# Loading the first key tiles through transposing DMAs instead of transposing them on the matrix engine

## The chip, the cores and the metric

The kernel runs on one core of one Trainium2 chip. The metric is the device time of one execution in microseconds (us); a time below is the median of several executions. The time contains about 1.8 us outside the profiled span (before: 179.15 us for a span of 177.4 us in the profiled run).

Engine names: PE is the matrix engine (PEld is its weight load, which overlaps PE), DVE the vector engine, ACT the scalar engine, POOL the general one, SP the engine that issues most DMAs. A q behind a name (SPq) means its sequencer.

## The reference, cut to what matters

The input x has 2048 tokens of 512 features. A linear-attention block and a gated feed-forward block run on the same x and are mixed by a gate:

```python
qkv = x @ wqkv                              # 32 heads of 16
pq, pk = phi(q), phi(k)                     # phi(t) = where(t > 0, t + 1, exp(t)) + 1e-6
kv  = einsum("bhsd,bhse->bhde", pk, v)      # a sum over all 2048 tokens
z   = pk summed over the tokens
a   = (pq @ kv) / (pq . z + 1e-6) @ wo
b   = (silu(x @ w1) * (x @ w3)) @ w2
out = g * a + (1 - g) * b                   # g = sigmoid(x . gate_w)
```

The kernel does not compute v for every token. It sums XP = x^T phi(k) over the tokens and multiplies by wv afterwards. So x is needed in two layouts: feature-major (`xT`), as the weights side of the key, query and feed-forward matmuls, and token-major (`x_sb`), as the weights side of the XP matmuls. Nothing of the query or feed-forward part can be finished before the keys of all 16 tiles of 128 tokens are through, so the kernel starts with the keys.

## The kernel before: the parts that matter

The start works like this. Token-major x of tiles 0-1 comes first, as a copy. PE transposes these two tiles itself (eight matmuls against an identity), DVE and ACT copy the result to `xT`. All other tiles get `xT` by a transposing DMA. The first half of wk is issued on ACT's queue, so that it is under way at the same moment as x.

```python
    TF = 2
    x_first = x2d[0 : TF * P, :].rearrange("(p j) d -> p j d", j=TF)
    dq.dma_start(out=x_sb[:, 0:TF, :], in_=x_first)
    nc.scalar.dma_start(out=wk_sb[:, 0:2, :], in_=wqkv_r[:, 0:2, D : 2 * D])
    dq.dma_start(out=wk_sb[:, 2:4, :], in_=wqkv_r[:, 2:4, D : 2 * D])
    dq.dma_start(out=xT[:, :, TF * P : TB], in_=x2d[TF * P : TB, :], transpose=True)
    for tb in range(1, NTB):
        dq.dma_start(out=xT[...tiles of tb...], in_=x2d[...], transpose=True)
        dq.dma_start(out=x_sb[...], in_=x_r[...])
    # ... (wq, wr, wv, w1, w3, wo, w2 in this order on the same queue)

    emit_warm(TB, TB, TB, TB, TB, TB, P, P, P)      # matmuls on constants while the loads run
    # ...
    emit_xT(0); emit_xT(1)                           # PE transposes
    for kc, t in ((0, 0), (1, 0), (0, 1), (1, 1), (2, 0), (3, 0)):
        emit_k_mm(k0[t], t, kc)                      # first wk half for tiles 0 and 1 first
    # ... (rest of key tiles 0-3)
    for t in range(TPB, NT):                         # key tile t behind XP of tile t-4
        for u in range(n_xp, n_xp + (2 if t == NT - 4 else 1)):
            emit_xp(u, XP_ps)
            n_xp = u + 1
        emit_k(t)
```

A key tile is four matmuls of 128x512 into one PSUM tile, then phi: exp on ACT, two instructions on DVE. XP of a tile is four matmuls.

## Time and profile before

| | before |
|---|---|
| median of six executions | 179.93 us (179.27 to 180.15) |
| span of the profiled run | 177.4 us |
| PE busy | 172.9 us, 97% |
| first key matmul / first XP matmul | 4.56 us / 8.03 us |

The page's first part (busy us, share of the span, instructions) and the first line of its fourth part (the chain of waits that ended last) say that PE is the limit from one end to the other:

```profile
PE 172.9 (97%) x868; PEld 83.7 (47%) x884; DVE 117.7 (66%) x203; ACT 65.9 (37%) x124; POOL 63.2 (36%) x71
...
PE 97%; issue 1%; DVE 0%; DVEq 0%
```

So only two things can move the time: PE's work itself, and the moments at which PE cannot go on. The timeline of PE's first 9 us (start, duration, engine, line, what it writes and reads, how often; in brackets the idle time before it and what ended it):

```profile
0.84 3.04 PE L163 MATMUL warm<-const-bfloat16-1.0 128*128 128x512 bf16 x9 [0.84 <-PEq L473]
3.89 0.62 PE L176 MATMUL xTp<-ident,x_sb 128*128 128x128 bf16 x8
4.56 3.63 PE L186 MATMUL k<-wk_sb,xT 128*128 128x512 bf16 x16
8.03 1.03 PE L206 MATMUL XP<-pk_sb,x_sb 128*128 128x512 bf16 x4
```

The 16 key matmuls of tiles 0-3 start at 4.56 and XP follows at 8.03: 3.47 us, or 0.217 us from one matmul to the next. There is no hole. (The duration that the line shows for the group, 3.63 us, is 0.16 us longer than this: it runs to the end of the last matmul.)

The waits of PE's weight loads:

```profile
PEld L176 <- DMA x_sb<-in_A_x_dram: 0.3, 1, 0.3
PEld L186 <- DMA xT<-in_A_x_dram: 0.2, 1, 0.2
PEld L186 <- DVE xT L181: 0.2, 1, 0.2
PEld L206 <- DMA x_sb<-in_A_x_dram: 0.2, 1, 0.2
```

SP's issues in the first 7 us, then the time from issue to landing of four of the loads (the DMA view, each taken for the stretch in which the load was issued; the columns are what, queue, kind, how many, size, us to landing):

```profile
0.81 0.40 SPq L84 DMA_DIRECT2D x_sb<-in_A_x_dram  x1
1.27 0.41 SPq L86 DMA_DIRECT2D wk_sb<-in_A_wqkv_dram  x1
1.73 1.32 SPq L89 DMA_TRANSPOSE xT<-in_A_x_dram  x1
3.10 2.77 SPq L93 DMA_TRANSPOSE xT<-in_A_x_dram  x1
```

```profile
wk_sb<-in_A_wqkv_dram ACTq DMA_DIRECT2D x1, 256.0 KB, 3.6
x_sb<-in_A_x_dram SPq DMA_DIRECT2D x1, 256.0 KB, 3.0
wk_sb<-in_A_wqkv_dram SPq DMA_DIRECT2D x1, 256.0 KB, 4.0
xT<-in_A_x_dram SPq DMA_TRANSPOSE x1, 4.4
```

Here a copy of 256 KB holds SP for 0.40 to 0.41 us and lands 3.0 to 4.0 us after its issue began. A transposing DMA of two tiles holds SP for 1.32 us.

The trace has records of the clock that PE was granted. In this run the first record says full clock from 3.76 us on. Until then the matmuls of 512 columns start 0.43 us apart, afterwards 0.216 us: PE begins at half clock.

### The profile page before, as it was taken

The page shows a single profiled execution, that of the slowest core. Times are in us where ns is not written, and L with a number is a line of the kernel's source. Part 1 is how long each engine was busy: PE and PEld are TensorE (multiplying, and loading weights), DVE is VectorE, ACT ScalarE, POOL GpSimd, SP SyncE. Part 2 cuts the span into 40 slices and gives each one's busy share as a digit, 9 for nine tenths or more (in the row PEclk, how much of TensorE's full clock was granted, in tenths as well). Part 3 has the DMA queues.
Part 4 walks back from the last instruction along what each step waited for, and adds up shares of the span by engine and source line. Part 5 has one row for each costly group of instructions (what it writes and reads, how often), then busy time and mean ns, then how long its engine had stood idle before and what let it go on. Part 6 is the DMA issues. An engine that isn't in the chain of part 4 may idle for free.

```text
span 177.4 us, 2453 instructions
## 1 busy us (share of the span) xinstructions
PE 172.9 (97%) x868; PEld 83.7 (47%) x884; DVE 117.7 (66%) x203; ACT 65.9 (37%) x124; POOL 63.2 (36%) x71
## 2 busy tenths in 40 slices
PE   8999999999999999999999999999999999999993
PEld 3444444474445454444454544444545444444463
DVE  0596858898998637597876466978754668776000
ACT  3624324466433333333244333243434323341222
POOL 5197655958262323262003232710032328000000
PEclk9999999999999999999999999999999999999999
DMA  5999889951014011124000111230002022200011
GB/s 172 237 265 238 253 273 348 358 171 28 9 30 91 7 41 37 37 59 89 0 4 7 41 33 38 70 79 6 0 7 67 7 70 59 59 0 0 30 36 56
DMA packets 30252, 15.14 MB, mean 85 GB/s; under 512 B 20672, under 2 KB 30112, under 8 KB 30240
## 3 DMA queue, kind: packets, MB, share of 16 engines
q1 hardware_dynamic: 29968, 14.72, 30.8%
q10 hardware_dynamic: 272, 0.26, 0.4%
q8 instruction: 7, 0.11, 0.3%
q14 instruction: 5, 0.04, 0.1%
HBM read 8.42 MB, written 2.10 MB: 59 GB/s over the span
## 4 chain that ended last, share of the span: by engine, by line
PE 97%; issue 1%; DVE 0%; DVEq 0%
PE o_ps L357 19%; PE up_ps L320 19%; PE gate_ps L312 19%; PE o_ps L348 8%; PE XP L206 8%; PE q_ps L219 8%; PE k_ps L186 6%; PE r_ps L243 3%; PE k L186 2%; PE o_ps L352 2%; PE warm L163 2%; PE kvT_ps L418 1%; PE W_ps L440 0%; PE z_ps L431 0%; DVE xT L181 0%
## 5 line engine op out<-in xcount | busy, mean ns | idle before, releaser
L312 PE MATMUL gate_ps<-xT,w_sb 128*128 128x512 bf16 x157 | 40.7, 379 | 0.1
L320 PE MATMUL up_ps<-xT,w_sb 128*128 128x512 bf16 x157 | 40.6, 379 | 0.2
L227 POOL TENSOR_TENSOR qz<-pq,z_sb 128x512 f32<-128x512 bf16 x16 | 18.5, 1163 | 59.6 <-DVE pq L147 58.4
L325 ACT ACTIVATE th<-gate_ps 128x512 bf16<-128x512 f32 x40 | 23.9, 597 | 37.9 <-PE gate_ps L312 36.4
L357 PE MATMUL o_ps<-w_sb,hT 128*128 128x512 bf16 (+3 forms) x177 | 37.3, 355 | 0.2
L327 DVE SCALAR_TENSOR_TENSOR gs<-th,gate_ps 128x512 bf16<-128x512 bf16 x40 | 27.3, 683 | 5.6 <-ACT th L325 5.3
L330 DVE TENSOR_TENSOR hT<-up_ps,gs 128x512 bf16<-128x512 f32 x40 | 27.6, 691 | 3.7
L144 DVE TENSOR_SCALAR phi_m<-phi_e 128x512 bf16<-128x512 bf16 x32 | 14.1, 442 | 21.4 <-ACT phi_e L142 21.4
L357 PEld LDWEIGHTS <-hT 128*128 128x128 bf16 x180 | 16.8, 98 | 17.9
L320 PEld LDWEIGHTS <-w_sb 128*128 128x128 bf16 x160 | 15.6, 98 | 18.9
L312 PEld LDWEIGHTS <-w_sb 128*128 128x128 bf16 x160 | 15.6, 98 | 18.6
L362 ACT ACTIVATE o_out<-o_ps,omg 128x512 bf16<-128x512 f32 (+2 forms) x17 | 11.2, 659 | 30.8 <-PE o_ps L357 30.8
L292 POOL TENSOR_TENSOR pqn<-pq,rden 128x512 bf16<-128x512 bf16 x16 | 16.6, 1058 | 14.0 <-DVE rden L285 11.7
L196 POOL TENSOR_TENSOR pks<-pks,pk_sb 128x512 f32<-128x512 f32 x15 | 17.4, 1162 | 7.3 <-DVE pk_sb L147 6.7
L348 PE MATMUL o_ps<-W_sb,pqT 128*128 128x512 bf16 (+3 forms) x70 | 16.7, 354 | 0.1
L230 DVE TENSOR_REDUCE den<-qz 128x32 f32<-128x512 f32 x16 | 11.0, 685 | 8.6 <-POOL qz L227 8.5
L206 PE MATMUL XP<-pk_sb,x_sb 128*128 128x512 bf16 x62 | 16.2, 379 | 0.1
L219 PE MATMUL q_ps<-wq_sb,xT 128*128 128x512 bf16 x61 | 16.1, 379 | 0.1
L142 ACT ACTIVATE phi_e<-k_ps 128x512 bf16<-128x512 f32 x12 | 7.2, 597 | 14.4 <-PE k_ps L186 14.4
L142 ACT ACTIVATE phi_e<-q_ps 128x512 bf16<-128x512 f32 x16 | 9.6, 597 | 7.8 <-PE q_ps L219 6.7
L186 PE MATMUL k_ps<-wk_sb,xT 128*128 128x512 bf16 x48 | 12.3, 379 | 0.0
L147 DVE SCALAR_TENSOR_TENSOR pq<-q_ps,phi_m 128x512 bf16<-128x512 f32 x16 | 11.1, 691 | 0.5
(59 smaller groups left out, 116.7 us busy)
## 6 DMA issues: line engine op xcount, KB each, us to landing
w_sb<-in_B_w_dram SPq DMA_DIRECT2D x6, 640.0 KB, 8.8
out_dram<-o_out SPq DMA_DIRECT2D x15, 128.0 KB, 1.9
x_sb<-in_A_x_dram SPq DMA_DIRECT2D x2, 512.0 KB, 5.4
x_sb<-in_A_x_dram SPq DMA_DIRECT2D x1, 768.0 KB, 5.4
wq_sb<-in_A_wqkv_dram SPq DMA_DIRECT2D x1, 512.0 KB, 6.9
wv_sb<-in_A_wqkv_dram SPq DMA_DIRECT2D x1, 512.0 KB, 5.8
wo_sb<-in_A_wo_dram SPq DMA_DIRECT2D x1, 512.0 KB, 10.3
wk_sb<-in_A_wqkv_dram ACTq DMA_DIRECT2D x1, 256.0 KB, 3.6
```

Of the source, the lines that this page charges most:

```text
L186: nc.tensor.matmul(k_ps[:], lhsT=xT[:, kc, t * P : (t + 1) * P], rhs=wk_sb[:, kc, :], start=(kc == 0), stop=(kc == KC - 1),)
L196: nc.gpsimd.tensor_add(pks[:], pks[:], pk_sb[:, t, :])
L206: nc.tensor.matmul(XP_ps[dc][:], lhsT=x_sb[:, t, dc * P : (dc + 1) * P], rhs=pk_sb[:, t, :], start=(t == 0), stop=(t == NT - 1),)
L219: nc.tensor.matmul(q_ps[:], lhsT=xT[:, kc, ts_tok], rhs=wq_sb[:, kc, :], start=(kc == 0), stop=(kc == KC - 1),)
L227: nc.gpsimd.tensor_tensor(out=qz[:], in0=st[tb, "pq"][:, tt, :], in1=z_sb[:], op=ALU.mult)
L312: nc.tensor.matmul(gate_ps[:], lhsT=w1_sb[:, kc, fsl], rhs=xT[:, kc, tok_sl], start=(kc == 0), stop=(kc == KC - 1),)
L320: nc.tensor.matmul(up_ps[:], lhsT=w3_sb[:, kc, fsl], rhs=xT[:, kc, tok_sl], start=(kc == 0), stop=(kc == KC - 1),)
L325: nc.scalar.activation(out=th[:], in_=gate_ps[:], func=ACT.Tanh, scale=0.5)
L327: nc.vector.scalar_tensor_tensor(out=gs[:], in0=th[:], scalar=1.0, in1=gate_ps[:], op0=ALU.add, op1=ALU.mult)
L330: nc.vector.tensor_tensor(out=st[tb, "hT"][:, fc, :], in0=up_ps[:], in1=gs[:], op=ALU.mult)
L348: nc.tensor.matmul(o_ps[:], lhsT=st[tb, "pqT"][:, c, tsl], rhs=W_sb[:, c, a:b], start=(c == 0), stop=False,)
L357: nc.tensor.matmul(o_ps[:], lhsT=st[tb, "hT"][:, fc, tsl], rhs=w2_sb[:, fc, a:b], start=False, stop=(fc == FC - 1),)
```

## The change

The intent: no PE transposes, no identity, no copies out of PSUM for them. One queue (SP's) loads everything, in the order in which it is needed: tile 0 transposed, wk in two halves, tile 1 and tiles 2-3 transposed, then token-major x. Because token-major x now comes late, XP of tiles 0-3 is moved behind key tile 3, and key tiles 4, 5, 6 follow without XP between. Some later weight loads are merged.

```diff
-    dq.dma_start(out=x_sb[:, 0:TF, :], in_=x_first)
-    nc.scalar.dma_start(out=wk_sb[:, 0:2, :], in_=wqkv_r[:, 0:2, D : 2 * D])
-    dq.dma_start(out=wk_sb[:, 2:4, :], in_=wqkv_r[:, 2:4, D : 2 * D])
-    dq.dma_start(out=xT[:, :, TF * P : TB], in_=x2d[TF * P : TB, :], transpose=True)
-    for tb in range(1, NTB):
-        # ... xT of four tiles, then token-major x of four (the first time six) tiles
+    load_xT(0, 1)
+    for kcs in (slice(0, 2), slice(2, 4)):
+        dq.dma_start(out=wk_sb[:, kcs, :], in_=wqkv_r[:, kcs, D : 2 * D])
+    load_xT(1, 2)
+    load_xT(2, 4)
+    load_x(0, 2)
+    load_x(2, 4)
+    load_xT(4, 8)
+    load_x(4, 8)
+    load_xT(8, 12)
+    load_x(8, 16)
+    load_xT(12, 16)
     # ... (w3 and w2 in one DMA each instead of two)
-    emit_warm(TB, TB, TB, TB, TB, TB, P, P, P)
+    emit_warm(TB, TB, TB, TB, TB, TB, TB)
     # ... (emit_xT is gone)
-    # ... (key tiles 0 and 1 begun with the first wk half)
+    for t in range(TPB):
+        emit_k(t)
     XP_ps = [...]
-    n_xp = 0
+    for t in range(TPB):
+        emit_xp(t, XP_ps)
+    n_xp = TPB
     for t in range(TPB, NT):
-        for u in range(n_xp, n_xp + (2 if t == NT - 4 else 1)):
-            emit_xp(u, XP_ps)
-            n_xp = u + 1
+        if t >= TPB + 3:
+            emit_xp(n_xp, XP_ps)
+            n_xp += 1
         emit_k(t)
```

## The prediction

> **What bounds the kernel now.** The profile's engine table has the matrix engine (PE) busy 172.9 of 177.4 us (97%); DVE is next, 66%. The chain that ended last is PE for 97%. The waits view shows four waits of PE's weight loads on another engine or a DMA, 0.9 us together. So only PE's work, or when PE can start and go on, moves the time.

> **The start, by the timeline.** Nine warming matmuls 0.84 to 3.88; x of tiles 0-1 (issued 0.81) lands at 3.8; eight transposes from 3.89; first key matmul 4.56; key tiles 0-3 end at 8.19. The first wk half, on ACT's queue at 0.80, lands at 4.4, the second at 5.3.

> **Removed.** Eight PE transposes with the wait for their copies (3.89 to 4.56: 0.67 us), two DVE copies of 292 ns, two ACT copies of about 380 ns, the identity. The other matmuls keep their number. The warming now ends at about 3.85, as before.

> **Added and moved.** The wk halves now stand behind a transposing DMA on one queue. Issuing a transposing DMA of one 128x512 tile takes 1.22 us (pqT, SP's timeline), data moves after that for 0.8 us, and it lands 2.4 us after the issue began. A copy of 256 KB is issued in 0.41 us and lands 3.0 to 4.0 us after it, two others in flight. My estimate from these: issues at 0.81 (xT 0), 2.1 and 2.5 (wk), 3.0 (xT 1), 4.3 (xT 2-3), 5.6 and 6.2 (x), 6.8 (xT 4-7). Landings: xT 0 3.4; wk 4.7 and 5.3; xT 1 5.6; xT 2-3 7.1; x 0-1 8.4; xT 4-7 about 10.7. Key tiles 0-1 then end at about 6.6 (a hole of 0.8 us before the first, a small one between the halves), tiles 2-3 start at 7.1 and end at about 8.85: 0.65 us later than before. The saved transposes are inside that.

> XP of tiles 0-3 runs 8.85 to 12.3; xT 4-7 is there by then. Key tiles 4, 5, 6 follow without XP between, and XP of tile 4 comes two key tiles (1.73 us) after key tile 4; phi takes 0.60 (ACT) + 0.29 + 0.69 (DVE) and about 0.2 us between, sometimes over 2 us: a stall of 0.1 to 0.4 us. Later PE's order is the same.

> **Later loads.** The queue runs 1 to 2 us later. wq (landed 23.2, used 29.6), w1/w3 (used 37.9) and wo (used 41.6) have time to spare; merged w3 and w2 loads cost nothing.

> **Sum.** +0.65 + 0.25 - 0.2 (the x_sb wait before XP of tile 2 goes) = +0.7: **180.7 us, 8 in 10 between 179.9 and 182.2**. Faster by over 2%: 0.01; within 2%: 0.95; slower by over 2%: 0.04.

> **What would show it.** PE idle 3.85 to about 4.7, released by the wk DMA; a hole before key tile 2, released by xT; key tile 3 ending at 8.5 to 9.5; a short wait for pk before XP of tile 4; no DMA wait after 13 us; PE busy about 0.6 us less, span 0.7 more.

> **What would make it wrong.** The wk copies might start only when the transposing DMA has drained (between later xT and x loads the trace shows about 0.6 us of nearly idle DMA): +0.6. [...] here full clock begins at 3.76 us. [...] if they cool PE, early key tiles take twice as long: +1.5 us.

The sum, +0.65 + 0.25 - 0.2 = +0.7 us, stands as it was put on record; no term of it is cut. "They" are the holes that the changed start leaves in PE's work. The +1.5 us is the author's estimate. By the trace of before (0.43 us from one matmul to the next until 3.76 us, 0.216 us afterwards) it is what seven key matmuls at half clock would cost.

## More of the kernel before

The weight load of XP of tile 2 waits 0.20 us and starts at 11.35 us; XP of tile 2 starts at 11.48 us, which is 8.03 us plus exactly 16 matmuls of 0.216 us.

## The result and the profile after

| | before | after |
|---|---|---|
| median of six executions | 179.93 us (179.27 to 180.15) | 182.25 us (181.1 to 182.7) |
| ratio | | 1.0128 (95% interval 1.009 to 1.0166) |
| span of the profiled run | 177.4 us | 180.9 us |
| PE busy | 172.9 us | 174.4 us |
| first key matmul / first XP matmul | 4.56 / 8.03 us | 5.43 / 11.37 us |

A ratio here is the mean time of one kernel's runs over the mean of the other's runs of the same rounds, so it is not quite the ratio of the medians quoted beside it.

The change is slower, by 1.3%, and the measured 182.25 us lies just outside the predicted range of 179.9 to 182.2 us. PE is busy for longer than before although eight transposes are gone. The two lines of the page that answer to those above:

```profile
PE 174.4 (96%) x858; PEld 83.3 (46%) x874; DVE 116.7 (65%) x201; ACT 65.4 (36%) x122; POOL 63.2 (35%) x69
...
PE 94%; DMA 2%; SPq 1%; issue 1%; DVE 0%; DVEq 0%
```

A DMA and SP's sequencer are now on the chain that ended last. The timeline of PE shows where:

```profile
0.84 3.03 PE L164 MATMUL warm<-const-bfloat16-1.0 128*128 128x512 bf16 x7 [0.84 <-PEq L453]
5.43 0.59 PE L173 MATMUL k_ps<-wk_sb,xT 128*128 128x512 bf16 x2 [1.55 <-DMA wk_sb<-in_A_wqkv_dram]
6.33 0.59 PE L173 MATMUL k_ps<-wk_sb,xT 128*128 128x512 bf16 x2 [0.31 <-DMA wk_sb<-in_A_wqkv_dram]
7.15 4.38 PE L173 MATMUL k_ps<-wk_sb,xT 128*128 128x512 bf16 x12 [0.23 <-DMA xT<-in_A_x_dram]
11.37 3.62 PE L193 MATMUL XP<-pk_sb,x_sb 128*128 128x512 bf16 x16
```

There are three holes: one in front of the first key matmul, one between the wk halves, one in front of key tile 1. And there is something that is not a hole. The last twelve key matmuls take from 7.15 to 11.37 us, 4.22 us, where twelve of 0.216 us would be 2.59 us. Between 7.15 and 10.5 us they start 0.43 us apart: half clock again.

The loads: SP's issues, then from issue to landing for xT of tile 0, the wk halves, xT of tile 1, and xT of tiles 2-3.

```profile
0.81 1.29 SPq L82 DMA_TRANSPOSE xT<-in_A_x_dram  x1
2.15 1.08 SPq L91 DMA_DIRECT2D wk_sb<-in_A_wqkv_dram  x2
3.28 2.55 SPq L82 DMA_TRANSPOSE xT<-in_A_x_dram  x2
```

```profile
xT<-in_A_x_dram SPq DMA_TRANSPOSE x1, 2.7
...
wk_sb<-in_A_wqkv_dram SPq DMA_DIRECT2D x1, 256.0 KB, 3.2
...
wk_sb<-in_A_wqkv_dram SPq DMA_DIRECT2D x1, 256.0 KB, 3.5
...
xT<-in_A_x_dram SPq DMA_TRANSPOSE x1, 3.8
...
xT<-in_A_x_dram SPq DMA_TRANSPOSE x1, 3.6
```

So xT of tile 0 is there at 3.51 us, but the wk halves land at 5.39 and 6.29 us (4.42 and 5.25 before), xT of tile 1 at 7.10 and of tiles 2-3 at 8.08 us.

The granted clock, by windows chosen at the trace's clock records (full from 3.63, half from 7.05, full from 10.46 us; each stretch is 3.41 us long; the columns are length, then busy us and count of PE, PEld, DVE, ACT and POOL, then the clock, the DMA share and GB/s):

```profile
0.22:3.63 3.41, 2.79 (x7) 0.96 (x8) 0.17 (x1) 1.49 (x2) 1.97 (x9) 1.00 0.21 45
3.63:7.05 3.42, 1.43 (x5) 0.32 (x4) 0.00 (x0) 0.09 (x1) 0.00 (x0) 1.00 0.98 235
7.05:10.46 3.41, 3.31 (x8) 1.19 (x9) 1.71 (x4) 1.10 (x2) 0.61 (x1) 0.50 1.08 217
10.46:13.87 3.41, 3.41 (x17) 1.57 (x16) 2.70 (x5) 1.19 (x2) 1.97 (x2) 1.00 0.92 221
```

In the first window PE was busy for 82% and got the full clock for the next one. In the second it was busy for 42%, because of the holes, and got half clock for the third. The third was full of matmuls, and full clock came back. (The view prints 1.00 for the first window, which has no record yet; the spacing of 0.43 us shows that it was half.)

With this the two profiled spans can be compared piece by piece. Each piece is a difference of start times in the two timelines:

| piece | us |
|---|---|
| first key matmul later: 5.43 against 4.56 | 0.87 |
| hole between the wk halves: second matmul done at 5.86, third starts at 6.33 | 0.47 |
| hole before key tile 1: fourth done at 6.76, fifth starts at 7.15 | 0.39 |
| half clock: 4.22 us for twelve matmuls instead of 2.59 | 1.63 |
| first XP matmul to first query matmul: 21.75 us (11.37 to 33.12) against 21.58 (8.03 to 29.61); from there to the end both take 147.8 us | 0.17 |
| sum | 3.53 |
| difference of the spans, 180.9 - 177.4 | 3.5 |

The medians differ by 2.3 us only. This execution of the changed kernel was among its slowest (182.64 us), and this one of before among its fastest (179.15 us). How much of that spread is the clock, the experiments show in part.

### The profile page after: what moved, and what is told of

Same layout as the page of the kernel before. It is cut to its first block, busy times and chain, and to the rows that moved or that the text cites. A ratio compares the mean times of both kernels' runs of the same rounds, so it can differ in the third digit from the quotient of the medians.

```text
span 180.9 us, 2426 instructions
## 1 busy us (share of the span) xinstructions
PE 174.4 (96%) x858; PEld 83.3 (46%) x874; DVE 116.7 (65%) x201; ACT 65.4 (36%) x122; POOL 63.2 (35%) x69
## 4 chain that ended last, share of the span: by engine, by line
PE 94%; DMA 2%; SPq 1%; issue 1%; DVE 0%; DVEq 0%
PE up_ps L307 19%; PE o_ps L344 19%; PE gate_ps L299 19%; PE k_ps L173 8%; PE XP L193 8%; PE o_ps L335 8%; PE q_ps L206 8%; PE r_ps L230 3%; DMA xT<-in_A_x_dram 2%; PE o_ps L339 2%; SPq L82 1%; SPq L91 1%; PE kvT_ps L398 0%; PE W_ps L420 0%; DVE o_out L353 0%
## 5 line engine op out<-in xcount | busy, mean ns | idle before, releaser
L312 ACT ACTIVATE th<-gate_ps 128x512 bf16<-128x512 f32 x40 | 23.9, 597 | 37.9 <-PE gate_ps L299 36.4
L145 DVE TENSOR_SCALAR phi_m<-phi_e 128x512 bf16<-128x512 bf16 x32 | 13.6, 424 | 29.0 <-ACT phi_e L143 28.8
L173 PE MATMUL k_ps<-wk_sb,xT 128*128 128x512 bf16 x63 | 17.5, 410 | 2.1 <-DMA wk_sb<-in_A_wqkv_dram 1.9
L143 ACT ACTIVATE phi_e<-k_ps 128x512 bf16<-128x512 f32 x16 | 9.6, 597 | 22.1 <-PE k_ps L173 22.1
L173 PEld LDWEIGHTS <-xT 128*128 128x128 bf16 x64 | 6.6, 104 | 11.7 <-issue 4.3
```

The source lines that it names most:

```text
L143: e_ins = nc.scalar.activation(out=e[:], in_=ps, func=ACT.Exp)
L173: nc.tensor.matmul(k_ps[:], lhsT=xT[:, kc, t * P : (t + 1) * P], rhs=wk_sb[:, kc, :], start=(kc == 0), stop=(kc == KC - 1),)
L312: nc.scalar.activation(out=th[:], in_=gate_ps[:], func=ACT.Tanh, scale=0.5)
```

## The experiments

Theory: the change loses twice. Its loads arrive later (wk stands behind a transposing DMA, xT of tile 1 behind both), and the holes that this tears open keep PE at half clock or put it back there. Rivals: the loads alone; the new order of XP; the use of one queue, with or without transposing DMAs.

### The changed kernel again

No edit. Six executions.

> The changed kernel again, unedited, for its spread. Theory (loads late[...]): times fall in two groups, about 182.6 us where the profile shows a half-clock stretch of 3.4 us in the first 12 us, and about 181.1 to 181.9 us where it shows none; ratio to before 1.007 to 1.015. Rival (the whole loss is the late loads and the order of XP, the clock stretch is a by-product of the profiler): one group, no relation of the time to the granted clock.

Measured: 182.31 us (181.31 to 182.7), ratio 1.0138 (1.0109 to 1.0167). The twelve executions of the changed kernel are not in two groups; they fill the range from 181.1 to 182.7 us. The mean granted clock does not tell them apart either: it is 0.999 for one of 182.7 us. So both expectations failed in form. The trace of that execution says why. It has no clock record before 10.06 us, and its key matmuls start 0.43 us apart until then:

```profile
0.00:3.24 3.24, 2.40 (x6) 0.90 (x7) 0.17 (x1) 1.49 (x2) 1.98 (x9) 1.00 0.18 40
3.24:6.65 3.41, 1.86 (x5) 0.46 (x4) 0.00 (x0) 0.00 (x0) 0.00 (x0) 1.00 0.97 225
6.65:10.06 3.41, 3.41 (x9) 1.17 (x8) 1.21 (x3) 1.20 (x2) 0.61 (x1) 1.00 0.91 234
```

### More warming matmuls, no load moved

```diff
-    emit_warm(TB, TB, TB, TB, TB, TB, TB)
+    emit_warm(*[TB] * 14)
```

> The changed kernel with 14 warming matmuls instead of 7, so that PE is busy until about 5.35 us, when the first wk half lands; no load is moved. If the half-clock stretch comes from PE's hole of 1.55 us before the first key matmul, no execution shows it, key tile 3 ends at about 9.8 us, and the time is 181.0 to 181.5 us in every execution: 1.5 us under the changed kernel's slow group, the same as its fast group. Rival (loads alone): no change from the changed kernel.

Measured: 181.04 us, four executions within 180.98 to 181.07; ratio 1.0073 (1.0048 to 1.0099). The executions of the unedited changed kernel in the same job average 182.19 us, so filling the hole is worth 1.16 us on average, with every load as it was. The profile has no half-clock stretch after 5.16 us:

```profile
0.84 5.30 PE L164 MATMUL warm<-const-bfloat16-1.0 128*128 128x512 bf16 x14 [0.84 <-PEq L453]
5.99 3.86 PE L173 MATMUL k_ps<-wk_sb,xT 128*128 128x512 bf16 x16
9.68 2.54 PE L193 MATMUL XP<-pk_sb,x_sb 128*128 128x512 bf16 x11
```

The warming delays the first key matmul to 5.99 us, but that costs nothing: key tile 1 starts at 7.08 us, on the landing of its xT, as it did in the changed kernel (7.15). XP starts at 9.68 us. The first rival (loads alone) falls, and so does the rival that the profiler makes the half-clock stretch: the executions themselves became faster. The spread is gone as well.

### A hole in the kernel before, no load moved

```diff
-    emit_warm(TB, TB, TB, TB, TB, TB, P, P, P)
+    emit_warm(TB, TB, TB)
```

> The kernel before with three warming matmuls instead of nine: PE idles from about 2.1 to 3.9 us, no load and no other work is moved. If a hole before the first work costs clock time by itself, the full clock comes later (first key tiles with 0.43 us from one matmul to the next) and the time rises by 1 to 2.5 us over before, to 181 to 182.3 us, spread by execution. Rival (the hole costs nothing as long as the loads are the limit): 179.8 us as before.

Measured: 181.39 us (181.07 to 181.55) beside 179.25 us for before; ratio 1.0112 (1.0088 to 1.0136). This is the clock alone: the loads of the start land within 0.25 us of before's, the first key matmul is even at 4.53 us, and still XP starts 2.27 us later, at 10.30 instead of 8.03 us.

```profile
0.84 1.44 PE L163 MATMUL warm<-const-bfloat16-1.0 128*128 128x512 bf16 x3 [0.84 <-PEq L473]
3.70 1.03 PE L176 MATMUL xTp<-ident,x_sb 128*128 128x128 bf16 x8 [1.42 <-DMA x_sb<-in_A_x_dram]
4.53 5.93 PE L186 MATMUL k<-wk_sb,xT 128*128 128x512 bf16 x16
10.30 1.03 PE L206 MATMUL XP<-pk_sb,x_sb 128*128 128x512 bf16 x4
```

The hole of 1.4 us stands where nothing could have run. What it costs is paid later: the 16 key matmuls took 5.77 us instead of 3.47, with full clock only from 9.20 us on.

### The order of XP alone undone

```diff
-    for t in range(TPB):
-        emit_xp(t, XP_ps)
-    n_xp = TPB
+    n_xp = 0
     for t in range(TPB, NT):
-        if t >= TPB + 3:
-            emit_xp(n_xp, XP_ps)
-            n_xp += 1
+        for u in range(n_xp, n_xp + (2 if t == NT - 4 else 1)):
+            emit_xp(u, XP_ps)
+            n_xp = u + 1
         emit_k(t)
```

> The changed kernel with before's order of XP and key tiles (XP of tile t-4 in front of key tile t). The theory puts 0.25 us on the new order (the wait of XP of tile 4 for phi of key tile 4 at 17.2 us goes): time 0 to 0.3 us under the changed kernel, same two groups. Rival (the new order is the main loss): the time falls by 1 us or more. XP of tiles 0-1 may instead wait for token-major x, which lands at about 10 us: that would show before the first XP matmul.

Measured: 182.68 us (182.6 to 182.89), ratio 1.0164 (1.0134 to 1.0193): about 0.5 us slower than the unedited changed kernel, not faster. XP of tile 0 does not wait, but key tile 4 does, for 1.02 us:

```profile
10.43 1.03 PE L193 MATMUL XP<-pk_sb,x_sb 128*128 128x512 bf16 x4
12.48 1.04 PE L173 MATMUL k_ps<-wk_sb,xT 128*128 128x512 bf16 x4 [1.02 <-DMA xT<-in_A_x_dram]
```

In the new load order xT of tiles 4-7 lands late (12.76 us in the changed kernel's profile), and the 16 XP matmuls behind key tile 3 are what hides that. So the new order is not the loss; it is part of what keeps the loss small. It may also be why these four executions hardly differ: key tile 4 waits for that landing (12.43 us in this profile) whether the key tiles before it were fast or slow. My expectation of a small gain had looked only at the wait of XP of tile 4 that the order makes (0.25 us expected, 0.17 us measured).

### Both wk halves on ACT's queue

```diff
+    for kcs in (slice(0, 2), slice(2, 4)):
+        nc.scalar.dma_start(out=wk_sb[:, kcs, :], in_=wqkv_r[:, kcs, D : 2 * D])
     # ... (pre, load functions)
     load_xT(0, 1)
-    for kcs in (slice(0, 2), slice(2, 4)):
-        dq.dma_start(out=wk_sb[:, kcs, :], in_=wqkv_r[:, kcs, D : 2 * D])
```

> The changed kernel with both wk halves issued on ACT's queue at 0.8 us, as before did with the first half; xT stays alone on SP's. If the loss is wk standing behind a transposing DMA on one queue: first key matmul at about 4.5 us instead of 5.43, key tile 1 not waiting until 7.1, key tiles 0-3 ending at about 8 to 8.5 us (11.53 in the changed kernel's profile), no half-clock stretch, time 180.0 to 180.5 us. Rival (the loss is transposing x of tiles 0-3 by DMA at all, on whatever queue): xT still lands as late, key tile 3 still ends after 9.7 us, time over 181 us.

Measured: 181.36 us, with two executions at 180.44 and 180.54 and two at 182.17 and 182.66; ratio 1.0097 (1.0049 to 1.0145). The first wk half now lands at 3.60 us. But the first key matmul is no earlier: it starts at 5.62 us, for now xT of tile 0 is what comes late.

```profile
0.84 3.03 PE L164 MATMUL warm<-const-bfloat16-1.0 128*128 128x512 bf16 x7 [0.84 <-PEq L453]
5.62 3.63 PE L173 MATMUL k_ps<-wk_sb,xT 128*128 128x512 bf16 x16 [1.74 <-DMA xT<-in_A_x_dram]
9.08 1.24 PE L193 MATMUL XP<-pk_sb,x_sb 128*128 128x512 bf16 x5
```

After that there is no hole, so XP starts at 9.08 us instead of 9.68 (the filled kernel), and the two fast executions are 0.5 us under the filled kernel's 181.0. The hole in front has become longer, 1.74 us, and executions over 182 us are there again. In the profiled execution this hole lost no clock: all 16 key matmuls are 0.216 us apart. No execution over 182 us was profiled here, so their half clock is inferred, from the experiment that fills this hole too (below). The expectation was wrong about the first key matmul, and the reason was new: the packets of xT of tile 0 had moved by 3.67 us, but its completion came at 5.57 us. The second wk half ran beside it on the other queue and completed at 4.98 us. The next experiment tests whether that half held it up.

### Only the first wk half on ACT's queue

```diff
+    nc.scalar.dma_start(out=wk_sb[:, 0:2, :], in_=wqkv_r[:, 0:2, D : 2 * D])
     # ...
     load_xT(0, 1)
-    for kcs in (slice(0, 2), slice(2, 4)):
-        dq.dma_start(out=wk_sb[:, kcs, :], in_=wqkv_r[:, kcs, D : 2 * D])
+    dq.dma_start(out=wk_sb[:, 2:4, :], in_=wqkv_r[:, 2:4, D : 2 * D])
```

> The changed kernel with only the first wk half on ACT's queue at 0.8 us; the second stays on SP's behind xT of tile 0. In e1_wk_act the data of xT of tile 0 had moved by 3.67 us, but its completion came at 5.57, after that of the second wk half (4.98), which ran beside it on ACT's queue. If it is that copy which holds the completion up, xT of tile 0 now lands at 3.6 to 4.2 us, the first key matmul starts at 3.9 to 4.3 (5.62 in e1), with a hole of about 0.7 us before the second half (landing at 5.3 or so); key tile 3 still ends at 9 to 9.7 us, because xT of tile 1 (issued at 2.7) and tiles 2-3 come late. Time 180.5 to 181.5 us. Rival (any copy beside a transposing DMA delays it, whatever the order): xT of tile 0 lands after 5 us again.

Measured: 180.73 us (180.58 to 180.84), ratio 1.0059 (1.0032 to 1.0087). The DMA view of the stretch in which both were issued, first with both halves on ACT's queue, then with one:

```profile
xT<-in_A_x_dram SPq DMA_TRANSPOSE x1, 4.8
```

```profile
xT<-in_A_x_dram SPq DMA_TRANSPOSE x1, 3.3
```

The packets of tile 0 had moved at the same moment in both (3.65 and 3.67 us), yet it is complete at 4.13 us here and at 5.57 us there. In the trace 32 packets of 4 bytes follow the tile's data. Here they start at 3.13 to 3.65 us, there only at 4.18 to 4.36 us, while the copy's data ends at 4.35 us. From the last data packet to completion it takes 0.48 us with the copy issued later, 1.90 us with the copy running beside. So I take it that the second wk half on the other queue held the tile up, at least for a part; by what means, these two runs do not show. Nor do they show that it is all: there the copy itself was complete at 4.98 us, and the 0.59 us from then to 5.57 us stay open. The edit also moved xT of tile 1 away, which there is issued 1.33 us behind tile 0. Where it is issued as close behind without a copy on another queue ("wk in front of xT of tile 0", below), the time from last packet to completion is 0.76 us, so that alone does not make 1.90. The rest of the start is again bound by loads:

```profile
4.18 0.61 PE L173 MATMUL k_ps<-wk_sb,xT 128*128 128x512 bf16 x2 [0.20 <-DMA xT<-in_A_x_dram]
5.66 3.62 PE L173 MATMUL k_ps<-wk_sb,xT 128*128 128x512 bf16 x14 [0.88 <-DMA wk_sb<-in_A_wqkv_dram]
9.40 0.82 PE L193 MATMUL XP<-pk_sb,x_sb 128*128 128x512 bf16 x3
```

The hole in front of the keys has shrunk to 0.2 us, and no execution is over 182 us: all four lie within 0.26 us. That the one follows from the other is argued; there is still a hole of 0.88 us between the wk halves. This is the best of the versions that keep the change's idea, if one goes by the mean.

### wk in front of xT of tile 0, on the one queue

The filled kernel (14 warming matmuls) with one more edit:

```diff
-    load_xT(0, 1)
     for kcs in (slice(0, 2), slice(2, 4)):
         dq.dma_start(out=wk_sb[:, kcs, :], in_=wqkv_r[:, kcs, D : 2 * D])
+    load_xT(0, 1)
     load_xT(1, 2)
```

> The kernel e2_fill (14 warming matmuls, so no clock loss) with one edit: on the one queue both wk halves are issued before xT of tile 0. Theory (a copy issued behind a transposing DMA pays its 1.3 us of issue and its data): wk lands at about 3.6 and 5.0 us, xT of tile 0 is issued at 1.8 and lands at about 4.7 to 5.2, the first key matmul is at about 5.2 to 5.5, without a hole between the halves; time 180.4 to 180.9, under e2_fill's 181.04. Rival (order on the queue does not matter, only the bytes in front of key tile 1 do): 181.0.

Measured: 181.46 us (181.11 to 181.59), ratio 1.0116 (1.0092 to 1.014), so no gain over the filled kernel. wk lands at 3.67 and 4.66 us and there is no hole between the halves, as expected. And xT of tile 0 lands at 5.35 us, so everything for key tile 0 is there 1.1 us earlier than in the filled kernel, where the second wk half lands at 6.45 us. That gains next to nothing: the 14 warming matmuls end at 5.9 us in this profile, and xT of tiles 2-3 lands at 7.76 us (7.87 in the filled kernel), so that the key tiles end hardly earlier. Then token-major x of tiles 0-1 landed only at 10.05 us, and XP of tile 0 waited for it:

```profile
5.93 3.78 PE L173 MATMUL k_ps<-wk_sb,xT 128*128 128x512 bf16 x16
10.10 1.25 PE L193 MATMUL XP<-pk_sb,x_sb 128*128 128x512 bf16 x5 [0.39 <-DMA x_sb<-in_A_x_dram]
```

The expected 0.1 to 0.6 us did not come. The order of the two on the one queue does not decide the time here.

### Both wk halves on ACT's queue and the hole filled

The edits of two experiments above together:

```diff
+        nc.scalar.dma_start(out=wk_sb[:, kcs, :], in_=wqkv_r[:, kcs, D : 2 * D])
-        dq.dma_start(out=wk_sb[:, kcs, :], in_=wqkv_r[:, kcs, D : 2 * D])
-    emit_warm(TB, TB, TB, TB, TB, TB, TB)
+    emit_warm(*[TB] * 14)
```

> e1_wk_act (both wk halves on ACT's queue) with 14 warming matmuls. Both repairs together: key tile 3 ends at about 9.1 us as in e1's profile, no slow executions; 180.2 to 180.6 us in all. What then remains over before (0.4 to 0.8 us) is xT of tile 0 landing at 5.6 us and XP of tile 4 waiting 0.2 us. If e1's slow executions (182.2 and 182.7) were not the clock, they stay.

Measured: 180.94 us (180.41 to 181.36), ratio 1.009 (1.0058 to 1.0121). The executions above 182 us are gone, which puts them down to the clock (four executions each); the mean is no better than the filled kernel's. In this profile the 14 warming matmuls end at 6.0 us, as late as xT of tile 0 (5.93). An execution in which full clock comes still later is then held up by the warming itself. This is argued from the profile; I did not vary the number of warming matmuls.

### One queue in the kernel before

```diff
-    nc.scalar.dma_start(out=wk_sb[:, 0:2, :], in_=wqkv_r[:, 0:2, D : 2 * D])
+    dq.dma_start(out=wk_sb[:, 0:2, :], in_=wqkv_r[:, 0:2, D : 2 * D])
```

> The kernel before with its first wk half on SP's queue, behind the copy of x of tiles 0-1: one queue, but a copy and not a transposing DMA in front. Theory (it is the transposing DMA in front that holds wk up: 1.3 us of issue, then its data): wk is issued at 1.3 and 1.7 us and lands at about 4.4 and 5.3 us; the first key matmul starts at 4.6 to 4.8, key tile 3 ends at 8.0 to 8.3; 179.6 to 180.0 us, within the spread of before. Rival (one queue is what costs): first key matmul after 5.2 us, 180.4 us or more.

Measured: 180.04 us (179.64 to 181.02) beside 180.0; ratio 1.0033 (0.9985 to 1.008), so no clear difference. wk lands at 4.41 and 5.22 us, the first key matmul is at 4.52 and the first XP matmul at 8.02 us: the start is before's to a few hundredths. The time that SP spends on issuing one more copy (0.41 us for a copy of 256 KB in before's profile) was not missed. So one queue is not what makes the start late. That leaves the transposing DMAs in the queue: in the changed kernel's start three of them hold SP for 1.2 to 1.3 us each. This is argued from the timelines; moving the first of them behind wk, and nothing else, did not help (above).

One thing behind the start did change: the DMA that brings token-major x of tiles 2-7 lands at 11.97 us instead of 11.30, and XP of tile 2 starts at 12.02 instead of 11.48. Here the wait for it is a real hole, and it makes up the 0.55 us by which this profile's span (178.0 us) is longer. The interval leaves room for such a loss.

### The changed idea at its best

First wk half on ACT's queue; xT of tiles 0-1 in one transposing DMA; the second wk half behind it; key tiles 0 and 1 begun with the first half; XP of tile 4 one key tile later.

```diff
+    nc.scalar.dma_start(out=wk_sb[:, 0:2, :], in_=wqkv_r[:, 0:2, D : 2 * D])
-    load_xT(0, 1)
-    for kcs in (slice(0, 2), slice(2, 4)):
-        dq.dma_start(out=wk_sb[:, kcs, :], in_=wqkv_r[:, kcs, D : 2 * D])
-    load_xT(1, 2)
+    load_xT(0, 2)
+    dq.dma_start(out=wk_sb[:, 2:4, :], in_=wqkv_r[:, 2:4, D : 2 * D])
     # ...
-    for t in range(TPB):
+    for kc, t in ((0, 0), (1, 0), (0, 1), (1, 1), (2, 0), (3, 0)):
+        emit_k_mm(k01[t], t, kc)
+    # ... (phi of tile 0, the rest of tile 1 and its phi)
+    for t in range(2, TPB):
         emit_k(t)
     # ...
-        if t >= TPB + 3:
+        for _ in range(0 if t < TPB + 4 else 2 if t == NT - 4 else 1):
             emit_xp(n_xp, XP_ps)
             n_xp += 1
```

> The changed idea at its best by what the runs show: first wk half on ACT's queue, xT of tiles 0-1 in one transposing DMA (one issue of 1.3 us instead of two), the second wk half behind it, key tiles 0 and 1 begun with the first half as before did, and XP of tile 4 one key tile later. Theory: xT of tiles 0-1 lands at about 4.2 to 4.5 us, the second half at about 5.3, xT of tiles 2-3 at about 6.7; key tile 3 ends at about 8.5 to 8.7 us (8.03 before), XP of tile 4 does not wait, and no window of the clock is idle enough to lose it: 179.9 to 180.4 us, within 0.5 us of before, still not faster. Rival (DMA transposes lose at least 1 us whatever the order): 180.8 or more.

Measured: 180.6 us, four executions at 180.35 to 180.65, two at 181.91 and 182.45; ratio 1.0085 (1.0043 to 1.0127). xT of tiles 0-1 landed at 4.61 us, a little later than expected, and the second wk half at 6.28 instead of 5.3 us. XP starts at 9.10 us. It is better than the change in four of six executions and still about 1.3 us over before's fastest runs. The profiled execution (180.35 us) has holes of 0.74 us in front of the keys and 0.63 us between the wk halves, both in the window from 3.72 to 7.13 us. PE was busy for 60% of it (2.05 of 3.41 us) and kept the full clock (42% in the window after which the changed kernel lost it). The two long executions were not profiled; that they lost the full clock is likely but not shown. The rival (about 1 us is lost whatever the order) came closer than my theory.

### The kernel before without the two waits that its profile shows

Second wk half on ACT's queue; token-major x of tiles 2-3 ahead of xT of tiles 4-7.

```diff
-    dq.dma_start(out=wk_sb[:, 2:4, :], in_=wqkv_r[:, 2:4, D : 2 * D])
+    nc.scalar.dma_start(out=wk_sb[:, 2:4, :], in_=wqkv_r[:, 2:4, D : 2 * D])
     # ... (xT of tiles 2-3)
+    dq.dma_start(out=x_sb[:, TF:TPB, :], in_=x_r[:, TF:TPB, :])
     for tb in range(1, NTB):
         # ... (xT of tb)
-        x_ts = slice(TF if tb == 1 else tb * TPB, (tb + 1) * TPB)
+        x_ts = slice(tb * TPB, (tb + 1) * TPB)
```

> The kernel before with its second wk half moved to ACT's queue and token-major x of tiles 2-3 loaded ahead of xT of tiles 4-7, to take away the two holes that before's profile shows (0.2 us in front of key tile 2, 0.2 to 0.3 us in front of XP of tile 2). 0.2 to 0.4 us faster than before if nothing else shifts: 179.4 to 179.6 us; the spread of before may hide it. Rival: the wk half on ACT delays x of tiles 0-1 and nothing is won.

Measured: 179.87 us (179.38 to 180.6) beside 179.25; ratio 1.0038 (1.0012 to 1.0064). Nothing was won; it is even slower by 0.4%, clear of noise. Both waits were weight-load waits without a hole in PE's stream, as shown above, so there was nothing to win. In the profile of this version full clock came only at 6.59 us and XP starts at 9.12 us, which is where most of its 180.6 us comes from; why its average is higher stays open. No version that I ran beats the kernel before.

## Why the prediction was wrong

The direction was right, and so were most of the waits that it named. The step that failed is the sum, in two terms: the key part, put at +0.65 us, measured +1.73 us because the loads landed later than estimated, and the clock, put at 0 and left among the risks, measured 1.63 us in the profiled run. Predicted were +0.7 us in all, measured +2.3 us (medians).

| step | predicted | measured |
|---|---|---|
| xT of tile 0 lands | 3.4 us | 3.51 us |
| wk halves land | 4.7 and 5.3 us | 5.39 and 6.29 us |
| xT of tile 1 / tiles 2-3 lands | 5.6 / 7.1 us | 7.10 / 8.08 us |
| key part, without the clock | +0.65 us | +1.73 us (0.87 + 0.47 + 0.39) |
| clock | 0, named as a risk of +1.5 | 1.63 us in the profiled run |
| XP of tile 4 waits for phi | +0.25 us | +0.17 us |
| wait for x before XP of tile 2 goes | -0.2 us | 0: it was no hole |
| later loads | no cost | no cost (21.75 against 21.58 us from XP to the first query matmul, the wait above included) |

1. **The landings were mis-sized.** The prediction quoted 3.0 to 4.0 us from issue to landing for the copies of before, and then used 2.6 and 2.8 us for wk, as if the two loads before it were not there. The result was 3.2 and 3.5 us, and the second half was also issued 0.29 us later than estimated (2.79 us), since the first copy held SP for 0.58 us. For xT of tile 1 it used 2.6 us, near the 2.4 us that it quotes for a transposing DMA later in the kernel; with 512 KB of wk in front it was 3.8 us. This term was 0.65 us in the sum and measured 1.73 us. The filled kernel supports the size: without the clock loss its first XP matmul is 1.65 us later than before's (9.68 against 8.03).

2. **The clock was put among the risks, and it belonged in the sum.** The prediction took its holes to be too short to cost clock; what it went by was not shown by any trace. A hole of 1.55 us, with two small ones behind it, was enough: the first two and most of the third fell into one window, 3.63 to 7.05 us, of which PE was busy for 42%, and half clock followed until 10.46 us. The hole of 1.74 us in the profile with both wk halves on ACT's queue lost nothing, so here the length of one hole did not decide it. That it matters where a hole falls is my reading. The experiments put numbers on it. In the job with both, the changed kernel averages 182.19 us, with the hole filled 181.03 us, before 179.72 us and its fastest execution 179.08 us. If the fastest execution of before lost nothing, then the loads, with the 0.17 us of the new order, cost 1.95 us (181.03 - 179.08), the clock costs the changed kernel 1.16 us on average, and it costs before 0.64 us (179.72 - 179.08), so the change pays 0.52 us more of it: together 2.47 us, the difference of the means. That before pays at all is an inference, supported by an edited copy of it (the last experiment above): with the same nine warming matmuls, full clock came at 6.59 us in its profile instead of 3.76, and that execution took 180.6 us.

3. **The -0.2 us was a misreading** of a weight load's wait as a hole of PE. Experiment and timeline both say so.

4. **What held:** PE idle until the wk DMA, a hole before a key tile that waits for its xT (tile 1; tile 2 was predicted), the short wait at XP of tile 4 (pk of tile 4 is ready at 17.53 us, XP starts at 17.59), no cost of the merged loads. Key tile 3 ended at 11.53 us and not at 8.5 to 9.5. "PE busy about 0.6 us less" failed, because half-clock matmuls count as busy: 174.4 us instead of 172.9.

What remains open: why xT of tile 1 took 3.8 us in the change. Its data began to move at about 5.3 us, when the wk packets were nearly through, 0.8 us after its issue had ended; I did not separate the queueing from the DMA's own latency.

## What to carry to other kernels

At the start of a kernel, compare two ways of loading by when the last operand of each matmul group lands, with everything that is queued in front included. A layout change that is free of PE's time may still cost more than a transpose on PE costs, when that transpose fits into the wait for another operand (here 0.67 us for the eight transposes before the change, 3.89 to 4.56 us, and a start that is 1.73 us later, clock aside, without them). Keep PE's stream full until the real work begins, with matmuls on constants if need be: a hole before the work can be paid a second time, in clock (2.1 us in the kernel before with its hole, by medians). Too much filling can itself hold up the work, as two profiles above suggest (warming until 5.9 and 6.0 us). And read a wait of the weight loads against the starts of the matmuls before calling it a loss.

## What these runs measured of the clock and of issue times

- Windows of 3.41 us, counted back from a clock record, and what followed. Windows at half clock of which PE was busy for 82% (changed kernel, 0.22 to 3.63 us), 84% (XP-order experiment, 5.03 to 8.44 us) and 86% (before, 0.35 to 3.76 us) were followed by full clock; those busy for 61% (the hole in before, 2.37 to 5.79 us) and 70% (the changed kernel run again, up to 3.24 us; XP-order experiment, 1.61 to 5.03 us) were not. No run lies between. At full clock, a window busy for 60% kept it (the changed idea at its best, 3.72 to 7.13 us), one busy for 42% lost it for 3.41 us (changed kernel, 3.63 to 7.05 us).
- The changed kernel run again started XP 1.56 us later than with its hole filled (11.24 against 9.68 us), 0.9% of its span of 181.0 us. The whole change is worth 1.3%, so a forecast of this size can't leave the clock out.
- The mean granted clock that the profile views print leaves out the stretch before the first record: it was 0.999 for an execution (the changed kernel run again) whose matmuls started 0.43 us apart until 10.06 us. The distance between matmul starts shows it.
- Issuing a transposing DMA held SP, in the first 20 us of the profiles before and after the change, for 1.20 and 1.29 us for one tile of 128x512, 1.30 and 1.32 us for two, and 2.77 to 5.39 us for four; a copy of 256 KB on the same queue held it for 0.40 to 0.58 us.
